# Attention slots beside a matmul stage: transposes and value products set later, evictions issued ahead of conversions, first slots a step later

## The chip, the cores and the metric

The kernel runs on one core of a Trainium2 chip. The metric is the device time of one execution in microseconds (us), the median of several executions. The engines meant below are TensorE (PE, matrix products), VectorE (DVE), ScalarE (ACT), GpSimd (POOL) and SyncE (SP, which here only issues DMAs). Each engine takes its instructions in the order in which they were written for it; semaphores hold an instruction back until its operands are there.

## The reference, cut to what matters

Three blocks follow one another. The first is attention over chunks of 32 queries with 8 memory keys, 16 keys to the left and 8 to the right; the two others are gated products without a nonlinearity. All is float32.

```python
scores = scale * np.matmul(q_c, k_full.transpose(0, 1, 3, 2))
scores = scores - np.max(scores, axis=-1, keepdims=True)
a = np.exp(scores)
a = a / (np.sum(a, axis=-1, keepdims=True) + 1e-09)
out[:, :, c_start:c_end] = np.matmul(a, v_full)
...
a = x @ w1;  b = x @ w2;  h = a * b @ w3;  return h @ w_out          # 3072 tokens, 512 -> 1024 -> 512
...
a = x @ w_a; b = x @ w_b; return (a * b @ w_out)                     # 512 -> 1536 -> 512
```

## The kernel before

**Units and slots.** Attention is cut into 64 units: one batch, 96 queries, half of the heads. A unit `u` goes through eight steps: scores on TensorE (`a_scores`, tile `sc`), the maximum on VectorE (`a_max`, `mx`), the exponentials on ScalarE (`a_exp`, `t`), the normalisation (sums on VectorE, `sm`, and the multiplication on GpSimd, `a_norm`), four transposes on TensorE (`a_trans`, `pt`), their eviction on ScalarE (`a_pt`, tile `p2`, which the traces call `p`), the value product on TensorE (`a_pv`, `xp`, for two units at once, at the odd one) and the split of the result into a high and a low part (`a_x`, `xt`: high on ScalarE, low on VectorE). `slots_of(u)` gives each step a slot number. The scores of unit `u` stand in slot 3u; before the change the transposes stand in slot 3u+5 plus up to six more for the early units, the eviction one slot behind, the value product two behind the transposes (three for units 0 to 9) and the split one more. `attn_slot(n)` issues the next n slots; within a slot the older unit's steps come first. So the slots are one list, and what is written around them decides how they lie among other work.

**Stage one (17 to 96 us): `w3 @ w_out`.** The two weights are multiplied first. Weights come from memory as 64-bit numbers. A call of `w_tick` converts: two scalings of one block on ScalarE (L378, L379) and, for the block before it, three integer operations on VectorE (L383 to L385). Blocks 0 to 7 are needed by steps k = 0 to 7 of the first half; blocks 8 to 11 hold two steps of the second half each. The loop over `order` runs two halves of four PSUM banks (`wps`); in each half steps k = 0 to 5 run over the banks m = 0 to 3, and then steps 6 and 7 bank by bank, and `w_evict` moves each finished bank out (high part on ScalarE, L570, low part on VectorE, L571, tile `wo`). The second half reuses the same four banks in the same order, so its first product into a bank waits for that bank's eviction. After every second product a tick or slots, or both, are issued.

**Stage two (96 to 510 us): the first gated block for 512 tokens at a time, `ti` = 0 to 4 here.** For each of eight feature blocks m, `ab_step` runs 12 matmuls into `psA` and 12 into `psB`; VectorE multiplies the two (`gv`, L635) and ScalarE and GpSimd split the product (`g`). Then come the `psY` products. Between every 12 matmuls `between()` issues first a tick (in `ti` = 0: 16 blocks of `w1` and `w2` are still to be converted, for psA and psB of the coming m) or a step of the preparation of the next weights (tiles `cs`, `co`), and then as many slots as bring the counter to its due value: `NEED[ti]` slots must be out before `ti` starts, since its input `xt` must be complete. There are 24 such places in each `ti`. Before the change 30 or 36 slots fall on them.

**Buffers and queues.** `pt` and `xp` have one buffer each, `p2` has two. Loads of keys, queries and values go through the POOL queue up to unit 13 and through the SP queue afterwards; in the SP queue they stand among the loads of weights and the stores of `co`.

Of the kernel before, what the change touches and what calls it, by code (L numbers as in the profile page):

```python
# [17 lines left out]
GQ = 96  # L18
# [3 lines left out]
TT = 512  # L22
NT1 = B * S // TT
NU = B * NG * 2
NPLAIN = 22
NEARLY = 14
# [9 lines left out]
A0 = (1, 2)  # L36
# [7 lines left out]
def tile_attention_moe(  # L44
# [46 lines left out]
    def mm(o, l, r, first, last):  # L91
        nc.tensor.matmul(o, lhsT=l, rhs=r, start=first, stop=last)  # L92
# [43 lines left out]
    def a_load(u):  # L136
        if u >= NU:
            return
        a_mask(u, queue_of(u))
        a_qk(u, queue_of(u))  # L140
# [7 lines left out]
    def a_prep_hi(u):  # L148
        if u >= NU:
            return  # L150
        q, k = qbuf[u % 2], kbuf[u % 2]
        q2 = att.tile([P, HH, GQ], F32R, tag="q2", name="q2")
        k2 = att.tile([P, HH, 2, KW], F32R, tag="k2", name="k2")
        split_hi(k2[:, :, 0, :], k)
        split_hi(q2[0:D], q[0:D])
        prep[u] = (q2, k2)

    def a_prep_lo(u):
        if u >= NU:
            return  # L160
        q, k = qbuf[u % 2], kbuf[u % 2]
        q2, k2 = prep[u]
        split_lo(k2[:, :, 1, :], k, k2[:, :, 0, :])
        split_lo(q2[D:P], q[0:D], q2[0:D])
# [108 lines left out]


    def trans_slot(u):
        return 3 * u + 5 + max(0, (NEARLY - 2 - u) // 2)

    def slots_of(u):
        t, e = trans_slot(u), int(u < NEARLY - 4)
        return (  # L280
            (t + 3 + e, a_x),
            (t + 2 + e, a_pv),
            (t + 1, a_pt),
            (t, a_trans),
            (3 * u + 3, a_norm),
            (3 * u + 2, a_exp),
            (3 * u + 1, a_max),
            (3 * u, a_scores),
        )

    todo = {}
    for u in range(NU):
        for j, (s, stage_of) in enumerate(slots_of(u)):
            todo.setdefault(s, []).append((j, u, stage_of))
        s = trans_slot(u) - (4 if u < NEARLY - 4 else 1)
        todo.setdefault(s, []).append((len(slots_of(u)), u, a_v))
    acount = [-3]
    NSLOT = 3 * (NU - 1) + 9

    NEED = [3 * (2 * -(-TT * (i + 1) // GQ) - 1) + 9 for i in range(NT1)]  # L300

    def attn_slot(n=1):
        for _ in range(n):
            s = acount[0]
            if s >= NSLOT:
                return
            acount[0] += 1
            for _, u, stage_of in sorted(todo.get(s, []), key=lambda x: x[:2]):
                stage_of(u)

            if s % 3 == 0 and s // 3 + 1 > NPLAIN + 1:
                a_prep_lo(s // 3 + 1)
            if s % 3 == 2 and s // 3 + 2 > NPLAIN + 1:
                a_prep_hi(s // 3 + 2)
            if s % 3 == 0 and NPLAIN <= s // 3 + 1 <= NPLAIN + 1:
                a_prep_hi(s // 3 + 1)
            if s % 3 == 1 and NPLAIN <= s // 3 + 1 <= NPLAIN + 1:
                a_prep_lo(s // 3 + 1)
            if s % 3 == 2:
                if s // 3 + 2 <= NPLAIN + 1:  # L320
                    a_load(s // 3 + 2)
                if s // 3 + 3 >= NPLAIN + 2:
                    a_load(s // 3 + 3)
# [31 lines left out]
    def w_load():  # L355
        i = nload[0]
        if i < len(wsrc):
            tag = "raw64" if size[i] == 1 else "raw2"
            r, x = w_tile(i, tag, [P, size[i] * CH, 2])
            if r is not None:  # L360
                for c in range(2 if i == 0 else 1):
                    n = size[i] * CH // (2 if i == 0 else 1)
                    nc.sync.dma_start(
                        out=r[:, n * c : n * c + n, :].rearrange("p c w -> p (c w)"),
                        in_=wsrc[i][:, 2 * n * c : 2 * n * c + 2 * n],
                    )
                nload[0] += 1
                wraw.append((i, r, tag))
                return True
        return False  # L370

    def w_scale(r):

        l, h = r[:, :, 0], r[:, :, 1].bitcast(F32)
        nc.scalar.activation(h, h, AF.Copy, scale=2.0**-112)  # L378
        nc.scalar.activation(l, l, AF.Copy, scale=2.0**-29)  # L379
# [7 lines left out]
    def halves_of(i, *tiles):  # L387
        if i > 0:
            return [tiles]
        return [[t[:, CH * c : CH * c + CH] for t in tiles] for c in range(2)]  # L390

    def w_sum(i, r):
        kind, f = plan[i][:2]
        if kind == "w12":
            a, ax = w_tile(i, "dec", [P, CH])
            w_bits(a, r)
            return a.bitcast(F32), ax
        if f % 2 == 0:
            pairs["f"] = wpool.tile([P, 2, 2 * CH], U32, tag="w12", name="w3_f")
        a = pairs["f"][:, f % 2, :]  # L400
        for a1, r1 in halves_of(i, a, r):
            w_bits(a1, r1)
        if kind == "w3a":
            w3k[f], wo_f[f] = a[:, :CH], a[:, CH:]
        else:
            w3k[8 + 2 * f], w3k[9 + 2 * f] = a[:, :CH], a[:, CH:]
        return None, None

    def w_tick():

        if len(pipe[2]):
            i, a, ax, (d, f, w, hi, lo) = pipe[2].pop(0)
            nc.vector.tensor_tensor(lo, a, hi.bitcast(F32), ALU.subtract)
            live["dec"][ax] -= 1
            d[f] = w
        if pipe[1]:
            i, a, ax = pipe[1].pop(0)
            t = w_place(*plan[i][:3])
            nc.scalar.activation(t[3], a, AF.Copy)
            pipe[2].append((i, a, ax, t))  # L420
        if len(pipe[0]):
            i, r, tag = pipe[0].pop(0)
            a, ax = w_sum(i, r)
            live[tag][int(tag == "raw2")] -= 1
            if ax is not None:
                pipe[1].append((i, a, ax))
        if wraw:
            i, r, tag = wraw.pop(0)
            for (r1,) in halves_of(i, r):
                w_scale(r1)  # L430
            pipe[0].append((i, r, tag))
        while w_load():
            pass
# [6 lines left out]
    def w_new(pool, tag, n=None):  # L440
        return pool.tile([P, 2, CH], F32R, tag=tag, bufs=n, name=tag)

    def w_place(kind, m, c):

        if c == 0:
            pairs[kind] = wpool.tile([P, 2, 2 * CH], F32R, tag="w12", name="w12")
        w = pairs[kind][:, :, CH * c : CH * (c + 1)]
        v = pairs[kind].rearrange("p l (k j f) -> p l k j f", k=KD, j=2)
        return (w12s if c else {}), m, v, w[:, 0, :], w[:, 1, :]
# [118 lines left out]
    def w_evict(half, m):  # L568
        w = wsm[4 * half + m] = w_new(wpool, "wo")
        nc.scalar.activation(w[:, 0, :], banks[m], AF.Copy)  # L570
        nc.vector.tensor_tensor(w[:, 1, :], banks[m], w[:, 0, :].bitcast(F32), ALU.subtract)  # L571
# [3 lines left out]
    for half in range(2):  # L575
        banks = [psd.tile([P, 512], F32, tag="d", name="wps") for _ in range(4)]
        for k, m in order:
            mm(
                banks[m],
                w3k[8 * half + k].bitcast(F32)[:, P * m : P * m + P],  # L580
                wo_f[k].bitcast(F32),
                k == 0,
                k == 7,
            )
            if k < 6 and m % 2 == 0 or k == 6:
                continue

            if half == 0:
                if m == 1 or k == 7 and m == 3:
                    w_tick()  # L590
                attn_slot(A0[m // 2] * (k > 0) if k < 6 else 1)
            else:
                if k < 6:
                    if m == 3:
                        w_tick()
                    attn_slot(1 + (m == 3 or k % 2 == 0))
                else:
                    if m % 2 == 1:
                        w_tick()
                    if m < 2:  # L600
                        attn_slot()
            if k == 7 and m > 0:
                w_evict(half, m - 1)
        w_evict(half, 3)
    nc.sync.dma_start(out=mask_sb, in_=mask)
    del pairs["f"]
    wo_f.clear()
# [35 lines left out]
    def between():  # L643
# [10 lines left out]
        if ti < NT1 - 1:  # L654
            b = nstep[0] - NB * ti
            attn_slot(NEED[ti] + (NEED[ti + 1] - NEED[ti]) * b // NB - acount[0])

# [49 lines left out]
    for ti in range(NT1):  # L707
        last = ti == NT1 - 1
        gs = {}
        attn_slot(NEED[ti] - acount[0])  # L710
        if last:
# [18 lines left out]
        for n in (0, 2, 1, 3) if last else range(KD):  # L730
            psY = psd.tile([P, 512], F32, tag="d", name="psY")
            i = 0
# [284 lines left out]
```

## Time and profile before

| | before |
|---|---|
| median of 3 runs | 1122.23 us (1122.22, 1122.23, 1123.91) |
| the profiled execution | 1123.84 us, its span 1122.1 us |
| TensorE busy | 1098.8 us, 98% of the span |
| VectorE busy | 642.5 us, 57% |
| ScalarE busy | 515.3 us, 46% |
| GpSimd busy | 310.7 us, 28% |
| chain that ended last | TensorE 80%, VectorE 3%, issue 2%, ScalarE 2%, GpSimd 1% |

TensorE is the bound of the whole, so only its waits count; they are read in the waits of TensorE and in its timeline. An engine that is busy 57% of the span can still bind a stretch, so busy time is read by stretch. The clock that was granted to TensorE (1.00 is 2.4 GHz, 0.50 is 1.2 GHz) is read in the windows: it tells where matmuls ran at half their speed.

### The profile page before, as it was taken

The numbers are of one execution on the slowest core, as the hardware profiler recorded it, in microseconds if no ns is written. First come the engines' busy times: TensorE is split into PE (matmuls) and PEld (weight loads), VectorE is DVE, ScalarE is ACT, GpSimd is POOL, SyncE is SP. The second block draws the span as 40 slices with busy tenths as digits, with TensorE's granted clock in tenths as the row PEclk, the third lists the DMA queues.
The fourth block names the chain that finished last, engine by engine and source line by source line (L and its number), as shares of the span: only waits on it lengthen the run. The fifth ranks groups of instructions, "written<-read, shape, count | busy, mean of one in ns | idle before, by whom it ended". The sixth has DMA issues, their size and how long they took to land.

```text
span 1122.1 us, 15526 instructions
## 1 busy us (share of the span) xinstructions
PE 1098.8 (98%) x5354; PEld 875.6 (78%) x5354; DVE 642.5 (57%) x1342; ACT 515.3 (46%) x1299; POOL 310.7 (28%) x308
## 2 busy tenths in 40 slices
PE   8899999999999999999999999999999999999998
PEld 3466877887787888887877878888888888888887
DVE  6878956877987887864865564252232244222220
ACT  6777656666666756644543334232222223222210
POOL 2452232332332322321212233202233211232210
PEclk9999999999999999999999999999999999999999
DMA  8835445345346345435446455434334352344311
GB/s 298 294 117 163 138 139 185 120 150 171 125 149 196 127 135 160 144 116 197 172 172 229 169 188 187 171 102 169 132 135 180 144 178 89 146 144 185 132 38 37
DMA packets 61671, 174.55 MB, mean 156 GB/s; under 512 B 8022, under 2 KB 18080, under 8 KB 55577
## 3 DMA queue, kind: packets, MB, share of 16 engines
q1 hardware_dynamic: 48762, 102.38, 27.5%
q0 software_dynamic: 12544, 70.91, 17.6%
q8 instruction: 42, 0.69, 0.3%
q14 instruction: 36, 0.29, 0.1%
q10 hardware_dynamic: 287, 0.27, 0.1%
HBM read 139.97 MB, written 33.55 MB: 155 GB/s over the span
## 4 chain that ended last, share of the span: by engine, by line
PE 80%; DVE 3%; issue 2%; ACT 2%; POOL 1%; DMA 0%; DVEq 0%; ACTq 0%; POOLq 0%; SPq 0%
PE ps L803 29%; PE ops L92 17%; PE psY L92 10%; PE psA L92 10%; PE psB L92 10%; PE sc L92 2%; PE xp L92 2%; PE pt L230 1%; DVE dec L384 1%; ACT t L209 0%; POOL t L222 0%; DVE dec L385 0%; DVE xt L146 0%; POOL g L637 0%; ACT xt L143 0%
## 5 line engine op out<-in xcount | busy, mean ns | idle before, releaser
L803 PE MATMUL ps<-x,w 128*128 128x512 f32 x1512 | 349.5, 390 | 3.8 <-ACT tmp L815 3.8
L803 PEld LDWEIGHTS ps<-x,w 128*128 128x128 f32 x1512 | 283.4, 188 | 64.6 <-ACT tmp L815 5.9
L820 DVE TENSOR_TENSOR tmp<-ps,tmp 128x512 f32<-128x512 f32 x108 | 74.6, 691 | 245.0 <-PE ps L803 241.0
L92 PE MATMUL psA<-xt,w 128*128 128x512 f32 x576 | 145.8, 401 | 2.1 <-ACT xt L143 1.5
L702 POOL DMA_DIRECT2D w<-wc x72 | 40.1, 558 | 369.0 <-PE ps L803 368.8
L92 PE MATMUL psB<-xt,w 128*128 128x512 f32 x576 | 141.0, 393 | 0.0
L92 PE MATMUL psY<-g,wo 128*128 128x512 f32 x576 | 139.0, 393 | 0.0
L815 ACT ACTIVATE tmp<-ps 128x512 f32<-128x512 f32 x108 | 64.6, 598 | 146.8 <-PE ps L803 146.8
L222 POOL TENSOR_TENSOR t<-t,sm 96x512 f32<-96x512 f32 x64 | 81.5, 1274 | 175.0 <-ACT k L143 79.8
L92 PEld LDWEIGHTS psA<-xt,w 128*128 128x128 f32 x576 | 106.6, 190 | 26.9 <-ACT xt L143 2.5
L92 PEld LDWEIGHTS psY<-g,wo 128*128 128x128 f32 x576 | 105.6, 188 | 21.0
L92 PEld LDWEIGHTS psB<-xt,w 128*128 128x128 f32 x576 | 105.5, 188 | 20.9
L637 POOL TENSOR_TENSOR g<-gv,g 128x512 fp32r<-128x512 f32 x48 | 67.9, 1414 | 188.6 <-ACT g L636 174.5
L92 PE MATMUL ops<-wo,g 128*128 128x512 f32 x504 | 118.6, 389 | 0.0
L92 PEld LDWEIGHTS ops<-wo,g 128*128 128x128 f32 x504 | 94.6, 188 | 19.6
L826 ACT ACTIVATE g<-tmp 128x512 fp32r<-128x512 f32 x66 | 40.8, 633 | 130.5 <-DVE tmp L825 130.5
L827 POOL TENSOR_TENSOR g<-tmp,g 128x512 fp32r<-128x512 f32 x66 | 87.1, 1342 | 26.5 <-ACT g L826 26.0
L209 ACT ACTIVATE t<-t,mx 96x128 f32<-96x128 f32 x168 | 65.1, 390 | 14.0 <-DVE mx L194 13.9
L92 PE MATMUL ops<-fo,g 128*128 128x512 f32 x288 | 68.2, 389 | 0.0
L92 PE MATMUL wps<-w_f 128*128 128x512 f32 x128 | 60.9, 607 | 4.2 <-DVE w_f L385 2.3
L636 ACT ACTIVATE g<-gv 128x512 fp32r<-128x512 f32 x48 | 30.2, 629 | 72.1 <-DVE gv L635 72.1
L92 PEld LDWEIGHTS ops<-fo,g 128*128 128x128 f32 x288 | 54.1, 188 | 11.2
(83 smaller groups left out, 1318.5 us busy)
## 6 DMA issues: line engine op xcount, KB each, us to landing
w<-wc POOLq DMA_DIRECT2D x36, 1024.0 KB, 6.9
w<-wc POOLq DMA_DIRECT2D x36, 768.0 KB, 4.9
wc<-co SPq DMA_DIRECT2D x84, 256.0 KB, 2.3
raw<-in_wab SPq DMA_DIRECT2D x24, 512.0 KB, 4.3
kraw<-in_kt SPq DMA_DIRECT2D x42, 256.0 KB, 3.2
raw<-in_w SPq DMA_DIRECT2D x16, 512.0 KB, 3.7
raw<-in_w3a SPq DMA_DIRECT2D x7, 1024.0 KB, 9.1
vraw<-in_vw SPq DMA_DIRECT2D x50, 128.0 KB, 2.5
```

Of the source, the lines that this page charges most:

```text
L92: nc.tensor.matmul(o, lhsT=l, rhs=r, start=first, stop=last)
L209: nc.scalar.activation(t[:, h, :], src[:, h, :], AF.Exp, bias=mx[:, h : h + 1], scale=scale, accum_out=sm[:, h : h + 1],)
L222: nc.gpsimd.tensor_tensor(t, t, sm[:, :, None].to_broadcast([GQ, HH, KW]), ALU.mult)
L230: nc.tensor.transpose(pt[:, h, :], t[:, h, :], id_sb)
L636: nc.scalar.activation(g2[:, 0, :], gv, AF.Copy)
L637: nc.gpsimd.tensor_tensor(g2[:, 1, :], gv, g2[:, 0, :].bitcast(F32), ALU.subtract)
L702: nc.gpsimd.dma_start(out=t[:, c0:c1].bitcast(F32), in_=src[:, c0:c1])
L803: nc.tensor.matmul(ps, lhsT=w[:, i, a, k, :], rhs=xs[i][:, b, k, :], start=first and n == 0, stop=n == 5, skip_group_check=not first,)
L815: nc.scalar.activation(z, ps, AF.Copy)
L820: nc.vector.tensor_tensor(z, ps, y, ALU.add)
L826: nc.scalar.activation(g2[:, 0, :], z, AF.Copy)
L827: nc.gpsimd.tensor_tensor(g2[:, 1, :], z, g2[:, 0, :].bitcast(F32), ALU.subtract)
```

## The change

`trans_slot` puts the transposes of units 12 and up six slots behind their scores instead of five. `slots_of` now sets the value product three slots behind the transposes and the split four behind for all units but 10 and 11; before, that held for units 0 to 9 only, and the others had two and three. `NSLOT` and `NEED` follow from the table: each `NEED` but the first grows by two, so 32 slots instead of 30 fall into `ti` = 0 and the split that ends a block of tokens stays in the last slot before its due time. In stage one the slots start at k = 2 instead of k = 1, three slots later; the second half issues two slots at each place, 24 in the k < 6 part instead of 21, so the counter is the same (42) at its end. `w_evict` of a bank is issued in front of the tick and the slots of its place instead of behind them, and the second tick at the end of the first half stands behind the last eviction.

```diff
     def trans_slot(u):
-        return 3 * u + 5 + max(0, (NEARLY - 2 - u) // 2)
+        n = NEARLY - 2
+        return 3 * u + (6 if u >= n else 5 + (n - u) // 2)
     def slots_of(u):
-        t, e = trans_slot(u), int(u < NEARLY - 4)
+        t, e = trans_slot(u), int(u // 2 != NEARLY // 2 - 2)
...
-    NSLOT = 3 * (NU - 1) + 9
-
-    NEED = [3 * (2 * -(-TT * (i + 1) // GQ) - 1) + 9 for i in range(NT1)]
+    NSLOT = max(todo) + 1
+    NEED = [slots_of(2 * -(-TT * (i + 1) // GQ) - 1)[0][0] + 1 for i in range(NT1)]
...
+            if k == 7 and m > 0:
+                w_evict(half, m - 1)
             if half == 0:
-                if m == 1 or k == 7 and m == 3:
+                if m == 1:
                     w_tick()
-                attn_slot(A0[m // 2] * (k > 0) if k < 6 else 1)
+                attn_slot(A0[m // 2] * (k > 1) if k < 6 else 1)
             else:
                 if k < 6:
                     if m == 3:
                         w_tick()
-                    attn_slot(1 + (m == 3 or k % 2 == 0))
+                    attn_slot(2)
...
-            if k == 7 and m > 0:
-                w_evict(half, m - 1)
         w_evict(half, 3)
+        if half == 0:
+            w_tick()
```

VectorE at the seam of the two halves of stage one, before (`raw_275`, `raw_312`: blocks 9 and 10 of the weights; `wo<-wps`: evictions; `mx`, `sm`: maximum and sums of a unit):

```order
L571 TENSOR_TENSOR wo<-wps,wo 128x512
L383 TENSOR_SCALAR w_f<-raw_275 128x1024
L384 SCALAR_TENSOR_TENSOR w_f<-raw_275,w_f 128x1024
L385 ISA w_f<-raw_275,w_f 128x2048
L220 TENSOR_SCALAR sm<-sm 96x4
L221 RECIPROCAL sm<-sm 96x4
L571 TENSOR_TENSOR wo<-wps,wo 128x512 x2
L186 TENSOR_REDUCE mx<-sc 96x4
L187 TENSOR_SCALAR mx<-mx 96x4
```

VectorE at the same seam, now (`raw_254` is block 9):

```order
L571 TENSOR_TENSOR wo<-wps,wo 128x512 x2
L220 TENSOR_SCALAR sm<-sm 96x4
L221 RECIPROCAL sm<-sm 96x4
L571 TENSOR_TENSOR wo<-wps,wo 128x512
L383 TENSOR_SCALAR w_f<-raw_254 128x1024
L384 SCALAR_TENSOR_TENSOR w_f<-raw_254,w_f 128x1024
L385 ISA w_f<-raw_254,w_f 128x2048
L186 TENSOR_REDUCE mx<-sc 96x4
L187 TENSOR_SCALAR mx<-mx 96x4
```

The last evictions stood behind the conversion of block 9 and stand ahead of it now; the maximum, of unit 6 before and of unit 5 now, stands behind that conversion in both.

ScalarE at this seam, before (`p_446` is the evicted transposes of unit 3):

```order
L570 ACTIVATE wo<-wps 128x512 x2
L234 ACTIVATE p_446<-pt 128x384
L209 ACTIVATE t,sm<-sc,mx 96x128 x4
L378 ACTIVATE raw_366<-raw_366 128x1024
L379 ACTIVATE raw_366<-raw_366 128x1024
```

ScalarE, now (`p_454` is the evicted transposes of unit 3, `p_423` those of unit 2):

```order
L570 ACTIVATE wo<-wps 128x512 x2
L378 ACTIVATE raw_286<-raw_286 128x1024
L379 ACTIVATE raw_286<-raw_286 128x1024
L143 ACTIVATE xt<-xp 128x4x96
L234 ACTIVATE p_423<-pt 128x384
L209 ACTIVATE t,sm<-sc,mx 96x128 x4
L378 ACTIVATE raw_341<-raw_341 128x1024
L379 ACTIVATE raw_341<-raw_341 128x1024
L234 ACTIVATE p_454<-pt 128x384
```

The eviction of unit 3's transposes stood right behind the last bank evictions; now two scalings of a block and the exponentials of unit 5 are between them.

ScalarE in `ti` = 0, before (`p_1159` is unit 15's eviction, `g_1091` the split of the product of m = 3):

```order
L209 ACTIVATE t,sm<-sc,mx 96x128 x4
L234 ACTIVATE p_1159<-pt 128x384
L636 ACTIVATE g_1091<-gv 128x512
L419 ACTIVATE w_1139<-dec 128x512
L378 ACTIVATE raw_1113<-raw_1113 128x512
L379 ACTIVATE raw_1113<-raw_1113 128x512
```

ScalarE in `ti` = 0, now (`p_1192` is unit 15's eviction, `g_1096` the split of m = 3):

```order
L638 ACTIVATE g_1096<-gv 128x512
L419 ACTIVATE w_1146<-dec 128x512
L378 ACTIVATE raw_1118<-raw_1118 128x512
L379 ACTIVATE raw_1118<-raw_1118 128x512
L234 ACTIVATE p_1192<-pt 128x384
L209 ACTIVATE t,sm<-sc,mx 96x128 x4
L633 ACTIVATE av<-psA 128x512
```

Unit 15's eviction stood ahead of the split of m = 3 and stands behind it now, and behind a tick's three activations.

TensorE in `ti` = 0, now, at the value product that reads it (`w_982` is m = 4):

```order
L92 MATMUL psB<-xt,w_982 128x512 x12
L92 MATMUL xp<-p_1086,vraw 64x96 x4
L92 MATMUL xp<-p_1192,vraw 64x96 x4
L230 MATMUL pt<-id_sb,t 128x96 x4
L92 MATMUL sc<-kraw,qraw 96x128 x4
L92 MATMUL psA<-xt,w_1052 128x512 x12
```

Before, that product stood behind psA of m = 4 and alone; now value product, transposes and scores stand together behind psB of m = 4.

## Rows read from the trace of the kernel before

**Rows 1.** Waits of TensorE, whole span: us in total, times, longest.

```profile
PE pt L230 <- POOL t L222: 2.3, 3, 1.3
PE xp L92 <- ACT p L234: 2.2, 1, 2.2
PE sc L92 <- DMA qraw<-in_qt: 2.2, 1, 2.2
PE wps L92 <- DVE wo L571: 1.9, 1, 1.9
PE psA L92 <- ACT xt L143: 1.5, 3, 0.6
PE pt L230 <- ACT p L234: 0.9, 1, 0.9
```

**Rows 2.** Windows: length, PE, PEld, DVE, ACT, POOL busy, granted clock, DMA, GB/s.

```profile
17.00:42.00 25.00, 21.89 (x87) 11.92 (x86) 23.10 (x35) 19.31 (x47) 11.32 (x17) 1.00 0.88 302
94.00:141.00 47.00, 44.77 (x237) 35.77 (x236) 43.90 (x75) 32.84 (x84) 11.64 (x10) 0.96 0.45 143
56.00:59.00 3.00, 3.00 (x10) 1.09 (x10) 2.90 (x5) 2.20 (x9) 1.91 (x3) 0.50 0.55 187
114.00:117.00 3.00, 3.00 (x9) 2.35 (x8) 2.87 (x5) 1.84 (x4) 1.64 (x2) 0.50 0.69 224
```

**Rows 3.** Timeline of TensorE: start, us, line, instruction, count, idle before.

```profile
32.47 1.08 PE L92 MATMUL sc<-kraw,qraw 67*96 67x128 f32 x8 [2.20 <-DMA qraw<-in_qt]
...
55.35 3.20 PE L92 MATMUL wps<-w_f 128*128 128x512 f32 x4 [1.94 <-DVE wo L571]
...
60.97 1.88 PE L92 MATMUL wps<-w_f 128*128 128x512 f32 x4
62.69 0.50 PE L230 MATMUL pt<-id_sb,t 96*128 96x96 f32 x4
...
67.46 0.88 PE L92 MATMUL xp<-p,vraw 128*64 128x96 f32 x16
...
157.73 3.00 PE L92 MATMUL psY<-g,wo 128*128 128x512 f32 x12
```

**Rows 4.** Timeline of VectorE at the seam of the two halves.

```profile
51.23 0.68 DVE L383 TENSOR_SCALAR w_f<-raw 128x1024 uint32<-128x1024 uint32 x1
...
54.64 1.25 DVE L571 TENSOR_TENSOR wo<-wps,wo 128x512 fp32r<-128x512 f32 x2
55.81 0.68 DVE L186 TENSOR_REDUCE mx<-sc 96x4 f32<-96x512 f32 x1
```

**Rows 5.** Timeline of ScalarE at the same seam.

```profile
53.48 0.53 ACT L234 ACTIVATE p<-pt 128x384 f32<-128x384 f32 x1
56.80 0.36 ACT L209 ACTIVATE t<-sc,mx 96x128 f32<-96x128 f32 x1 [2.79 <-DVE mx L187]
...
58.19 1.16 ACT L378 ACTIVATE raw<-raw 128x1024 f32<-128x1024 f32 x1
```

**Rows 6.** Timeline of VectorE in `ti` = 0: the product of m = 3.

```profile
130.47 0.68 DVE L635 TENSOR_TENSOR gv<-psB,av 128x512 f32<-128x512 f32 x1
```

**Rows 7.** Timeline of ScalarE around it.

```profile
129.87 0.49 ACT L234 ACTIVATE p<-pt 128x384 f32<-128x384 f32 x1
131.18 0.63 ACT L636 ACTIVATE g<-gv 128x512 fp32r<-128x512 f32 x1 [0.82 <-DVE gv L635]
...
132.24 0.65 ACT L378 ACTIVATE raw<-raw 128x512 f32<-128x512 f32 x1
```

**Rows 8.** Timeline of TensorE at the seam of `ti` = 0 and 1.

```profile
180.45 0.63 PE L92 MATMUL sc<-k,q 128*96 128x256 f32 x4
...
183.75 0.88 PE L92 MATMUL xp<-p,vraw 128*64 128x96 f32 x16
184.56 0.55 PE L230 MATMUL pt<-id_sb,t 96*128 96x96 f32 x4
185.52 3.43 PE L92 MATMUL psA<-xt,w 128*128 128x512 f32 x12 [0.42 <-ACT xt L143]
```

## The prediction

> **What bounds the kernel now.** I read the waits of TensorE first, because TensorE is busy nearly all the time and only its waits can be won. Those that the change can touch sum to 11.0 us: transposes for GpSimd 2.3, a value product for ScalarE 2.2, scores for a load 2.2, a bank for its eviction 1.9, psA for its input 1.5, a transpose for ScalarE 0.9 [rows 1]. Then the windows: behind the eviction wait and behind the value product wait the granted clock is 0.50 (1.2 GHz) for some 3.4 us [rows 2], of which I show 3 us each; half speed over 3.4 us loses 1.7 us. So about 14.5 us hang on these waits. Next, the other engines in the same stretches: VectorE is busy 23.1 of 25 us between 17 and 42 us, and 43.9 of 47 us between 94 and 141 us [rows 2]. That is the point to see: the waits of TensorE lie just where VectorE has nearly no idle time. A wait that another full engine causes cannot be removed by an order alone; it can only move.
>
> Times below count from the start of the profiled span (1122.1 us; that execution took 1123.84 us, so 1.7 us lie around the span). The three timed runs stand at 1122.2, 1122.2 and 1123.9, a distance of one such stretch at half clock, so the profile belongs to the upper kind.
>
> **Stage one.** What moves: slots start one step later, evictions go ahead of ticks, 24 slots instead of 21 in the second half. No instruction is added or removed. I follow VectorE and ScalarE, with these prices: a conversion on VectorE 3.2 (from 51.23 to the sums and evictions that end at 55.81) [rows 4], an eviction 0.6 [rows 4], a maximum 0.8 (up to 1.2 at some), sums 0.3, exponentials 1.4 to 1.5 [rows 5], the two scalings of a block 2.1 to 2.3 [rows 5], the eviction of transposes 0.5 [rows 5].
>
> VectorE begins block 4 at 22.4, when its scaling is done, as before. Blocks 4 to 7 with three maxima and two sums (12.9 + 3.2 + 0.6) end at 39.1. Sums and the maximum of unit 3 follow (40.6), then its exponentials (42.3), its transposes' eviction (42.8), bank 0's eviction on ScalarE and VectorE (44.05), block 8 (47.3), the maximum of unit 4 (48.1), its exponentials (49.75), the evictions of banks 2 and 3 (51.9). TensorE asks for banks 2 and 3 at 51.4 and 52.3: **the eviction wait of 1.94 goes**, with a margin of 0.4.
>
> What is late next stands on the order of ScalarE. Block 9 ends at 55.15, the maximum of unit 5 behind it at 55.95, its exponentials at 57.6, the scalings of the tick behind them at 59.7, and only then comes the eviction of unit 3's transposes, done at 60.2. Before, that eviction ran at 53.48 [rows 5]. TensorE wants it for the value product of units 2 and 3 at 57.0: two products take 1.72 [rows 3], eight pairs of them, four scores, four transposes and one value product from the late scores of unit 3 (36.4) on. So **a new wait of about 3.2 us** follows the removed one. The scores' wait for their load does not go either: the load stands in the POOL queue behind a normalisation whose sums come 3.9 us later (a conversion and a maximum are ahead of them), and TensorE comes only 3.4 us later (the four products that now go ahead), so 2.2 becomes some 2.7 to 3.0. Small waits of 0.3 to 0.9 follow at two transposes. By the third value product I count 69.65 against 67.46 before [rows 3], with two products (1.72) more behind it: **0.5 us behind**, although before had a stretch at half clock there. The bounds: 1.5 us ahead if only half of the new waits comes, 1.2 us behind if the new wait drops the clock, of whose 1.7 the waits that follow absorb about 1.
>
> From 70 us on TensorE waits for nothing in both, until the first psA at 96.5. VectorE, though, reaches its last eviction about 1.1 us later than before (99.9 for 98.8), since the maximum of unit 11 stands behind a tick now; 0 to 2 us is what I allow.
>
> **`ti` = 0.** Here the lengthened distances act: the value product that waited 2.2 [rows 1] now stands two places behind its eviction, and the transposes that waited 1.3 have a slot more. Both waits go, and with the clock's 1.7 this is 5.3 us. But VectorE works through the same list without a gap up to gv of m = 3, which began at 130.47 [rows 6]; 1.1 later it is 131.6. Unit 15's eviction ran at 129.87, ahead of the split of that product [rows 7]; now it stands behind the split and a tick. From gv: split at 132.3, one more activation and two scalings (131.18 to 132.24 for the first two, 0.65 for a scaling), eviction 134.5 to 135.0 [rows 7]. TensorE, without its old waits, asks for it at 130.3 (ten times 2.83 us of psA or psB from 96.5, four transposes, four scores, a value product). So **a wait of 4.7 us** stands where 5.3 were won, and a clock at half speed behind it is likely: 1.94 and 2.23 us of idle were each followed by one, while 2.20 us at 32.47 was not [rows 2, 3]. From that product on TensorE again binds: the first psY at 157.4, or at 159.1 with the clock's loss, against 157.73 [rows 3]. I take 159.1, **1.4 behind**.
>
> The Trainium skill ("TensorE: Matmul & The Clock Gate", section "Why this matters for your kernels") advises against idle gaps of several us between bursts, since the clock falls behind them. The rows show it falling after shorter gaps too, and not after each, so length alone doesn't decide; by the page as by my choice the 4.7 us gap costs a stretch, and the sum would be the same.
>
> **After `ti` = 0.** The two other transposes' waits, 0.95 together (2.3 less 1.3 [rows 1]), go, with three slots between normalisation and transposes. At a seam of two `ti` the split follows the value product, and psA waits for it: value product at 183.75, transposes at 184.56, psA at 185.52, with 0.42 shown as wait and another 0.4 inside its first twelve (3.43 for 2.9 to 3.0) [rows 8]. Now scores stand behind the transposes there, 0.47 each [rows 8]. They cover that much at four of the five seams: 1.9. Together **2.8 us**, with bounds 0 (ScalarE may be late with the split, having exponentials ahead) and 3.5.
>
> The costs I set at nothing: the loads of values in the SP queue come one slot later and now stand two slots, not three, behind the product that frees their buffer; stores wait behind them, and TensorE's distance to what those stores free covers it. If that cover goes, see the second rival. The table's other buffers keep their distances.
>
> **The sum.** 159.1, plus the rest of the span as before (1122.1 less 157.7, 964.4), less 2.8, is 1120.7; with 1.7 around the span 1122.4. Against the median of 1122.23 this is no change; a measurement of this kernel tells about 0.2% (2.2 us) from none.
>
> **The rivals.** (1) The waits go and come back smaller. Without the half clock behind the new wait in `ti` = 0 the sum is 1120.7, and with VectorE not 1.1 late 1119.6. If VectorE were no bound at all, the 14.5 us go outright: 1109. For it: TensorE may run up to 8 us ahead of VectorE's weights in `ti` = 0. Against: the order puts unit 15's eviction behind gv. Chance of under 1120.0: 0.30. (2) Slower: the SP queue. A value load that waits for TensorE holds back the stores of `co`, and ScalarE, in order, waits for their buffer with evictions behind it. Some 20 loads wait up to a slot (2.3 us) longer; it decides if ScalarE falls more than two slots behind TensorE. If one in four costs 0.8, this is 4 us, 1126.4. With both new waits' half clock and no gain at the seams 1125.2 comes out by another way. Together over 1124.5: 0.20. (3) The eviction wait stays, for lack of 0.4 us of margin: under 1 us, and inside the forecast.
>
> **How the numbers follow.** Forecast (no change): 0.50, its own range 1120.0 to 1124.5. Faster 0.30, slower 0.20. The range from 1117.5 to 1125.5 takes in the missing half clock, the bounds of VectorE's lag and half of the slower cases; it leaves out some 0.1 on each side.
>
> **What would show it.** Right: no wait of wps for wo; a wait of 2.5 to 4 us of xp for ScalarE near 57 to 60 us and one of 3 to 5 us near 130 to 135, a clock of 0.50 behind at least one; VectorE over 90% busy from 94 to 141; no waits of transposes for GpSimd; psA's waits at the seams shorter. Wrong: no wait of xp over 1 us before 157 us (then the time is below 1118), or ScalarE waiting longer for the stores of `co` and TensorE for ScalarE after 200 us (then above 1124).

## The result and the profile after

| | before | after |
|---|---|---|
| median, same chip | 1123.47 us (6 runs) | 1130.82 us (6 runs) |
| ratio | | 1.0072, 95% interval 1.0062 to 1.0083 |
| the profiled execution, its span | 1123.84, 1122.1 us | 1132.6, 1130.8 us |
| TensorE busy | 1098.8 us | 1102.1 us |
| first psA of `ti` = 0 | 96.54 us | 97.61 us |
| first psY of `ti` = 0 | 157.73 us | 159.15 us |
| from there to the end of the span | 964.4 us | 971.6 us |

The change makes the kernel slower by 0.7%, outside the predicted range of 1117.5 to 1125.5. The last three lines tell where: up to the first psY the two kernels stand 1.4 us apart, and behind it 7.3 us more are lost. The waits of TensorE after (as in [rows 1]; us in total, times, longest):

```profile
PE psY L92 <- ACT g L638: 3.4, 1, 3.4
PE xp L92 <- ACT p L234: 3.0, 1, 3.0
PE psY L92 <- POOL g L639: 2.6, 3, 1.0
PE sc L92 <- DVE mx L194: 2.3, 4, 0.6
...
PE sc L92 <- DMA qraw<-in_qt: 2.0, 2, 1.6
...
PE sc L92 <- DVE mx L187: 1.6, 1, 1.6
...
PE pt L230 <- POOL t L222: 0.8, 1, 0.8
```

The eviction wait is gone, the waits of transposes for GpSimd went from 2.3 to 0.8, and the value product waits once, 3.0 us, in stage one. New are waits of psY for `g` of ScalarE and of GpSimd, 6.0 us together, and scores that wait for a maximum. Where they stand, in the timeline of TensorE after (as in [rows 3]):

```profile
35.06 1.08 PE L92 MATMUL sc<-kraw,qraw 67*96 67x128 f32 x8 [1.57 <-DVE mx L187]
...
59.08 0.77 PE L92 MATMUL xp<-p,vraw 128*64 128x96 f32 x8 [3.02 <-ACT p L234]
...
127.56 1.99 PE L92 MATMUL sc<-kraw,qraw 67*96 67x128 f32 x8 [1.60 <-DMA qraw<-in_qt]
...
322.99 4.96 PE L92 MATMUL psY<-g,wo 128*128 128x512 f32 x21
331.34 0.50 PE L92 MATMUL psY<-g,wo 128*128 128x512 f32 x1 [3.38 <-ACT g L638]
332.86 1.22 PE L92 MATMUL psY<-g,wo 128*128 128x512 f32 x2 [1.02 <-POOL g L639]
...
357.89 2.98 PE L92 MATMUL psA<-xt,w 128*128 128x512 f32 x12
```

And the windows of after (as in [rows 2]: length, PE, PEld, DVE, ACT, POOL busy, granted clock, DMA, GB/s):

```profile
94.00:141.00 47.00, 44.60 (x230) 35.17 (x229) 43.89 (x76) 33.29 (x91) 11.25 (x9) 0.93 0.51 151
...
59.50:66.00 6.50, 6.50 (x25) 4.10 (x22) 4.69 (x7) 3.36 (x12) 5.01 (x8) 0.50 0.33 100
128.00:134.00 6.00, 6.00 (x19) 4.99 (x18) 5.67 (x10) 4.72 (x15) 1.43 (x3) 0.50 0.52 160
332.50:339.00 6.50, 6.14 (x19) 5.07 (x20) 6.30 (x19) 4.70 (x17) 1.63 (x2) 0.50 0.14 49
...
320.00:340.00 20.00, 15.60 (x76) 12.16 (x75) 19.18 (x53) 13.56 (x43) 6.01 (x6) 0.83 0.38 131
```

The last of these windows, before:

```profile
320.00:340.00 20.00, 20.00 (x125) 16.08 (x124) 18.26 (x53) 12.29 (x42) 5.76 (x4) 1.00 0.39 132
```

TensorE ran at 1.2 GHz behind the waits at 59.08, 127.56 and 331.34, for some 6.8 us each, where before had two such stretches of 3.4 us. From 320 to 340 us VectorE is busy 19.18 of 20 us while TensorE stands still for 4.4; before, TensorE was busy all of these 20 us. So 6.8 of the 7.3 us lie in one place: the psY products of `ti` = 2 took 34.9 us from the first psY to the next `ti` (322.99 to 357.89), before 28.1 (321.58 to 349.65). All other parts behind 159 us differ by 1 us or less each.

The order in which VectorE and ScalarE work there repeats with every pair of psA and psB in `ti` = 2. VectorE after (start, us, line, instruction, idle before it):

```profile
276.44 0.68 DVE L637 TENSOR_TENSOR gv<-psB,av 128x512 f32<-128x512 f32 x1
...
310.43 0.17 DVE L220 TENSOR_SCALAR sm<-sm 96x4 f32<-96x4 f32 x1 [0.23 <-ACT t L209]
...
310.95 0.69 DVE L146 TENSOR_TENSOR k<-kraw,k 128x512 fp32r<-128x512 f32 x1
311.68 1.28 DVE L146 TENSOR_TENSOR q<-qraw,q 64x384 fp32r<-64x384 f32 x1
312.99 0.56 DVE L146 TENSOR_TENSOR xt<-xp,xt 128x384 fp32r<-128x384 f32 x1
313.46 0.68 DVE L190 TENSOR_TENSOR t<-sc,mask_sb 96x512 f32<-96x512 f32 x1
...
315.02 0.68 DVE L637 TENSOR_TENSOR gv<-psB,av 128x512 f32<-128x512 f32 x1
...
317.95 0.17 DVE L220 TENSOR_SCALAR sm<-sm 96x4 f32<-96x4 f32 x1 [1.91 <-ACT t L209]
...
329.94 0.68 DVE L637 TENSOR_TENSOR gv<-psB,av 128x512 f32<-128x512 f32 x1
```

ScalarE after, in the same stretch:

```profile
315.74 0.63 ACT L638 ACTIVATE g<-gv 128x512 fp32r<-128x512 f32 x1 [2.88 <-DVE gv L637]
316.27 0.39 ACT L209 ACTIVATE t<-t,mx 96x128 f32<-96x128 f32 x1
...
322.80 0.63 ACT L638 ACTIVATE g<-gv 128x512 fp32r<-128x512 f32 x1 [1.96 <-DVE gv L637]
```

To read them together: sums, low parts of keys and queries, split, maximum, gv on VectorE; gv lets ScalarE make `g`; the exponentials stand behind `g`; and the sums wait for the exponentials. **These steps stand in one chain, each behind the one before**: from 310.43 to 317.95 one turn takes 7.5 us. VectorE waits 1.91 us in this turn; in others the preparation of the weights (`co`, `dec`) fills that time, and it is busy 47.7 of the 53.5 us from the first gv to the last. The eight gv of `ti` = 2 begin at 276.44 to 329.94, 7.6 us apart; before, they were 7.2 apart. TensorE's pair takes 6.95 (55.6 us from first psA to first psY, by 8), so it runs ahead until it needs the last `g`. Before, the exponentials stood ahead of `g` on ScalarE and ran beside VectorE's work on gv, and gv waited for TensorE twice, at 272.11 and at 314.30 (VectorE before):

```profile
302.09 0.68 DVE L635 TENSOR_TENSOR gv<-psB,av 128x512 f32<-128x512 f32 x1
308.78 0.68 DVE L635 TENSOR_TENSOR gv<-psB,av 128x512 f32<-128x512 f32 x1
314.30 0.69 DVE L635 TENSOR_TENSOR gv<-psB,av 128x512 f32<-128x512 f32 x1 [0.97 <-PE psB L92]
```

What made the round is `NEED`: 72, 102, 138 before, multiples of three, and 74, 104, 140 after. `ti` = 2 has 36 slots for 24 places, so one place takes one slot and the next two. Before, the place behind psA took scores and sums (slot 3u) and the one behind psB the maximum and the exponentials; after, the exponentials (3u+2) stand alone behind psA, and sums, scores and maximum all stand behind psB, ahead of gv.

### The profile page after: what moved, and what is told of

Read it like the earlier page. It is cut to its first block, busy times and chain, and to the rows that moved or that the text cites. A ratio compares the mean times of both kernels' runs of the same rounds, so it can differ in the third digit from the quotient of the medians.

```text
span 1130.8 us, 15527 instructions
## 1 busy us (share of the span) xinstructions
PE 1102.1 (97%) x5354; PEld 880.4 (78%) x5354; DVE 652.0 (58%) x1342; ACT 515.7 (46%) x1299; POOL 313.3 (28%) x308
## 4 chain that ended last, share of the span: by engine, by line
PE 66%; DVE 11%; ACT 7%; issue 5%; DMA 1%; POOL 1%; SPq 0%; DVEq 0%; ACTq 0%; POOLq 0%
PE ps L805 29%; PE ops L92 17%; PE psY L92 9%; PE psA L92 5%; PE psB L92 4%; ACT t L209 3%; DVE q L146 2%; DVE gv L637 1%; DVE t L190 1%; DVE t L194 1%; DVE dec L384 1%; PE sc L92 1%; ACT k L143 1%; DVE co L146 1%; PE pt L230 1%
## 5 line engine op out<-in xcount | busy, mean ns | idle before, releaser
L92 PE MATMUL psA<-xt,w 128*128 128x512 f32 x576 | 143.5, 398 | 1.5 <-DVE xt L146 0.9
L222 POOL TENSOR_TENSOR t<-t,sm 96x512 f32<-96x512 f32 x64 | 85.1, 1330 | 196.5 <-ACT k L143 100.2
L92 PEld LDWEIGHTS psY<-g,wo 128*128 128x128 f32 x576 | 108.3, 191 | 29.5 <-ACT g L638 3.8
```

Source lines behind the costliest of these rows:

```text
L222: nc.gpsimd.tensor_tensor(t, t, sm[:, :, None].to_broadcast([GQ, HH, KW]), ALU.mult)
```

## The experiments

All times are medians against the kernel before on the same chip. "Behind psY" is the span less the start of the first psY of `ti` = 0; "`ti` = 2" runs from its first psA to that of `ti` = 3. Both are read from the timeline of TensorE in the one profiled execution of each run, so they need not add up to the ratio; that of the run with the table, NEED + 1 and evictions in front took 1124.20 us, 4.6 above its median. NEED + 1 means that each due value but the first is one later.

| run | ratio, 95% | first psY | behind psY | `ti` = 2 |
|---|---|---|---|---|
| before | | 157.73 | 964.4 | 84.2 |
| after | 1.0072 [1.0062, 1.0083] | 159.15 | 971.6 | 90.5 |
| table alone | 1.0047 [1.0034, 1.0059] | 155.98 | 971.4 | 90.3 |
| stage one alone | 1.0029 [1.0017, 1.0040] | 159.34 | 964.5 | 84.3 |
| after, NEED + 1 | 1.0000 [0.9991, 1.0009] | 160.22 | 962.2 | 84.0 |
| before, NEED + 2 | 1.0015 [1.0007, 1.0024] | 155.82 | 966.8 | 87.3 |
| table, NEED + 1 | 0.9979 [0.9970, 0.9988] | 155.64 | 961.9 | 84.0 |
| after, gv first | 1.0333 [1.0315, 1.0351] | 161.15 | 996.0 | 89.0 |
| after, places swapped | 1.0068 [1.0055, 1.0081] | 158.16 | 970.1 | 88.2 |
| table, NEED + 1, evictions in front | 0.9971 [0.9963, 0.9980] | 157.62 | 964.8 | 84.5 |
| the same, seam slots first | 0.9934 [0.9921, 0.9948] | 158.95 | 957.4 | 81.7 |
| after, queries on GpSimd | 0.9999 [0.9990, 1.0008] | 157.49 | 963.1 | 82.0 |

**The table alone, stage one alone.** The diff of the change, split in two: `trans_slot`, `slots_of`, `NSLOT` and `NEED` in the one, the loop of stage one in the other.

> The new table of slots (and NEED, NSLOT by it) with stage one as before. Three theories on the 7.3 us that are lost behind the first psY (971.65 us from there to the end, 964.3 before). RING: each NEED behind the first grew by two, so another third of the slots now falls on the place behind psA; between two gv VectorE's sums, splits and maximum, ScalarE's g and its exponentials then wait for one another in one ring of some 7.5 us, longer than the 6.9 us of the pair psA and psB in ti = 2. DISTANCE: transposes, value product and scores now stand in one slot, and this heap costs, wherever the places are. CARRIED: the lag comes from stage one and is never made up. RING and DISTANCE: 1128 to 1131 us, behind the first psY 970 to 972, psY waiting for g of ScalarE by some 3 us near 331. CARRIED: 1122 to 1125, 964 to 966 behind the first psY.

> The edits of stage one alone (first slots one step later, evictions in front), with the table of slots as before. RING and DISTANCE: 1121 to 1125 us, from the first psY to the end 963 to 966, no psY waiting for g by over 1 us. CARRIED: 1128 to 1131, 970 to 972 behind the first psY. By all three no wait of wps for wo near 55, and a wait of xp for ScalarE of about 3 us near 59.

The table alone took 1127.61 us (1122.83 for before) and has the wait of psY for `g` (3.4 us), with TensorE 1.8 us *earlier* at the first psY than before; the edits of stage one alone took 1126.01 without that wait. So nothing is carried over from stage one, and CARRIED falls. One number missed: stage one alone came out 1 us above what I wrote. Its span is only 1.7 us longer than that of the profiled execution of before, and each has one stretch at half clock in stage one (before at 56 to 59 us [rows 2]). Two other runs with stage one as before had none there and reached the first psA at 94.9 and 95.3 us; with the edited stage one it is 97.1 to 98.2 in six runs. The edits cost 2 to 3 us against an undisturbed stage one, and the clock accounts for about as much: the six have 3.4 to 10.2 us at 0.50 there, which is 1.7 to 5.1 us lost.

**The due values one and two later.** After, with the due values multiples of three again:

```diff
     NEED = [slots_of(2 * -(-TT * (i + 1) // GQ) - 1)[0][0] + 1 for i in range(NT1)]
+    NEED = [n + (i > 0) for i, n in enumerate(NEED)]
```

and before, with the values of the change (the same line with `n + 2 * (i > 0)`, the table as it was).

> The changed kernel with each NEED but the first raised by one (75, 105, 141, 171): the distances of the table stay, and the slots stand at the places behind psA and psB as before the change, since the due values are multiples of three again. RING: 1121 to 1125 us, 962 to 966 behind the first psY, no wait of psY for g over 1 us near 331. DISTANCE and CARRIED: 1128 to 1132, 970 to 972 behind the first psY.

> The kernel before with each NEED but the first raised by two (74, 104, 140, 170, as the change has them): old distances, stage one as before, the other third of the slots behind psA. RING: 1126 to 1131 us, 968 to 972 behind the first psY, and in ti = 2 gv of VectorE and g of ScalarE wait for each other in turn. DISTANCE and CARRIED: 1121 to 1125, 963 to 966 behind the first psY.

The first is as RING said: 1122.65 us, 962.2 behind psY, no wait of psY for ScalarE. The distances are those of the change, so DISTANCE falls. The second speaks against RING by its time, 1124.39 us, which the two others allowed, and for none by the 966.8 us behind psY. But its trace has the round of the kernel after (ScalarE and VectorE, before with NEED + 2):

```profile
311.14 0.63 ACT L637 ACTIVATE g<-gv 128x512 fp32r<-128x512 f32 x1 [3.38 <-DVE gv L636]
...
313.35 0.17 DVE L220 TENSOR_SCALAR sm<-sm 96x4 f32<-96x4 f32 x1 [1.91 <-ACT t L209]
```

but TensorE is held back by it in small pieces, at value products two slots behind their transposes (TensorE, the same run):

```profile
284.33 0.55 PE L92 MATMUL xp<-p,vraw 128*64 128x96 f32 x8 [0.21 <-ACT p L234]
300.07 0.55 PE L92 MATMUL xp<-p,vraw 128*64 128x96 f32 x8 [1.80 <-ACT p L234]
316.27 0.55 PE L92 MATMUL xp<-p,vraw 128*64 128x96 f32 x8 [0.72 <-ACT p L234]
```

2.7 us in three waits, and `ti` = 2 takes 3.1 us more than before. The gv stand 7.7 us apart, as after. Behind the wait of 1.80 the clock fell as well, for some 3.4 us (its window, the same run):

```profile
301.00:304.00 3.00, 3.00 (x8) 2.34 (x7) 2.07 (x11) 1.20 (x3) 0.49 (x1) 0.50 0.01 5
```

From 320 to 340 us it stays at 1.00. So the round comes from the due values with either table, at a price of some 3 us; RING as I had written it was too simple. With the distances of the change the value products don't wait, so the lag is passed to TensorE only at psY, at once, and the clock falls behind that wait, for twice as long.

**Does it add up, and two edits meant to open the round.** The table and NEED + 1 with stage one as before; after, with gv and `g` issued ahead of the slots behind psB; after, with the due slots of `ti` = 2 rounded up, so that the place behind psA takes two slots and that behind psB one:

```diff
-        between()
         nc.vector.tensor_tensor(gv, psB[:, :TT], av, ALU.mult)
         ...
+        between()
```

```diff
-            attn_slot(NEED[ti] + (NEED[ti + 1] - NEED[ti]) * b // NB - acount[0])
+            attn_slot(NEED[ti] + ((NEED[ti + 1] - NEED[ti]) * b + (NB - 1) * (ti == 2)) // NB - acount[0])
```

> Stage one as before, the new table, each NEED but the first one later than the table gives it (75, 105, 141, 171). The runs so far: the table alone costs 4.8 us, stage one's edits alone 3.2, table and stage one with the later NEED nothing. If the costs add, as RING says (the later NEED takes the wait of psY for g away, whatever stage one does): 1118 to 1121 us, first psY at 155 to 157 us, 964 or less from there to the end. If the later NEED only helps where TensorE comes late from stage one (OFFSET: what counts is how far TensorE stands from VectorE, not which place a slot has): 1123 to 1128, with a wait of psY for g of 2 to 4 us near 328.

> The changed kernel with gv and its split g issued ahead of the slots behind psB instead of behind them. RING: gv no longer stands behind sums, splits and maximum, so exponentials and g no longer wait for one another: no wait of psY for g of ScalarE near 331, and 1122 to 1126 us. ScalarE now holds its evictions of transposes behind g while psB runs, up to 3 us, so waits of xp for p may come instead; with those on every pair as in the run with the old table and NEED two later (4.6 us in all), 1126 to 1129. OFFSET: as the changed kernel, 1129 to 1132.

> The changed kernel with the due slots of ti = 2 rounded up instead of down: the place behind psA takes two slots and that behind psB one, where it was one and two; nothing else moves. RING: this alone takes the ring apart (sums, splits of keys and queries behind psA, maximum behind psB with nothing but the split of xp ahead of it): ti = 2 takes 84 to 85 us instead of 90.5, 1123 to 1126 us. If the loss in ti = 2 is brought in from ti = 1 or from due values that are too early (OFFSET), ti = 2 stays at 88 or more and the time at 1128 to 1132.

The first came out as the sum: 1120.31 us against 1123.15, faster than both kernels; OFFSET falls, since TensorE arrives early here (155.64) and no psY waits for ScalarE. The other two missed what I had expected by RING, but the traces show that neither edit opened the round. With gv first the wait of psY for ScalarE shrinks to 0.2 us, and another round closes: gv waits for `av` (1.92 us at 306.34), which stands on ScalarE behind the exponentials, these wait for the maximum, and the maximum now stands behind gv. The gv are 7.9 us apart, scores wait for the maximum, 18.7 us in 14 waits, and `ti` = 1 to 3 take 5 to 9 us longer than before. With the places swapped VectorE and ScalarE keep the very order of the round, sums, low parts, maximum, gv, `g`, exponentials, sums; only TensorE's scores moved ahead of psB (VectorE, ScalarE and TensorE, places swapped):

```profile
314.12 0.68 DVE L637 TENSOR_TENSOR gv<-psB,av 128x512 f32<-128x512 f32 x1
...
317.04 0.17 DVE L220 TENSOR_SCALAR sm<-sm 96x4 f32<-96x4 f32 x1 [1.91 <-ACT t L209]
...
314.84 0.63 ACT L638 ACTIVATE g<-gv 128x512 fp32r<-128x512 f32 x1 [3.20 <-DVE gv L637]
...
314.34 0.69 PE L92 MATMUL sc<-k,q 128*96 128x256 f32 x4 [1.66 <-DVE mx L194]
329.25 0.68 PE L92 MATMUL sc<-k,q 128*96 128x256 f32 x4 [1.19 <-DVE mx L194]
```

The eight gv stand 7.8 us apart (274.24 to 329.03). The wait at psY of `ti` = 2 is gone, but TensorE meets the same round at the scores: from unit 22 on `sc` has one buffer, so the scores of a unit need the maximum of the one before. `ti` = 2 gained only 2.3 of 6.3 us. VectorE is busy just 44.8 of the 54.8 us between the first gv and the last, so a VectorE with too much to do doesn't explain the distance of the gv; the round does.

**The length of the round.** After, and for the twelve units whose scores fall into `ti` = 2 a step of 1.28 us of VectorE's part of the round goes to GpSimd; no other instruction moves:

```diff
-        split_lo(q2[D:P], q[0:D], q2[0:D])
+        if NEED[2] <= 3 * u < NEED[3]:
+            nc.gpsimd.tensor_tensor(q2[D:P], q[0:D], q2[0:D].bitcast(F32), ALU.subtract)
+        else:
+            split_lo(q2[D:P], q[0:D], q2[0:D])
```

> The changed kernel; for the twelve units whose scores fall into ti = 2 the low part of the queries (1.28 us on VectorE) is computed on GpSimd instead. The order of everything else stays. RING, in the form that the runs left: the round sums, splits of keys and queries, maximum, gv on VectorE, then g and exponentials on ScalarE takes 7.1 to 7.9 us, TensorE's pair some 6.9, so 1.28 less makes it shorter than TensorE's: no wait of psY for g of ScalarE near 331, ti = 2 takes 83.5 to 85.5 us instead of 90.5, 1123 to 1126 us. If the wait comes from anything but the length of that round (the heap of value product, transposes and scores in one place, a load, a store): ti = 2 stays above 88 us and the time at 1128 to 1132.

1122.68 us against 1122.66, 8.1 less than after; `ti` = 2 takes 82.0 us, less than the 83.5 that I had put as its lower end, and the time lies 0.3 under its range too. The gv of this run stand 6.9 us apart (274.25 to 322.64), no psY waits for ScalarE, and the clock stays at 1.00 (its window):

```profile
320.00:340.00 20.00, 19.75 (x112) 15.97 (x110) 15.08 (x50) 13.51 (x44) 9.16 (x8) 1.00 0.47 155
```

The order of the change with a round shorter than TensorE's pair loses nothing behind psY (963.1 us, 964.4 before). The heap of value product, transposes and scores, the loads and the stores stand where they stood, so they were not the cause. VectorE has less to do here as well (15.08 of 20 us); that this alone was not it is told by the run with the places swapped. Together they show the cause: the length of the round.

**Evictions in front, and the seam.** The table, NEED + 1 and, of stage one's edits, only the evictions issued in front; then also, at the last place of each `ti`, the slots ahead of the step of the weights' preparation:

```diff
         nstep[0] += 1
+        if ti < NT1 - 1 and nstep[0] == NB * (ti + 1):
+            attn_slot(NEED[ti + 1] - acount[0])
         if any(pipe) or wraw:
```

> As the run of stage one as before with the new table and the later NEED, and the bank evictions of stage one issued in front of the ticks and slots of their place, without the other edits of stage one (first slots and last tick where they were). What this tells is which edit of stage one costs the 3.2 us: if it is the later slots (the exponentials and scalings that come ahead of an eviction of transposes), this is 0 to 2 us faster than that run, without the wait of wps for wo of 1.9 to 2.0 near 55; if it is the evictions in front (they move the transposes' eviction back), it is 1.5 to 3.5 us slower than that run, with a wait of xp for ScalarE of 2 to 3.5 us near 57 to 60.

> The last run's kernel (stage one as before but for the evictions in front, the new table, the later NEED), and at the last place of each ti the slots issued in front of the step of the weights' preparation instead of behind it. In that run psA waited 2.3 us at 186.36 and 2.2 us at 351.96 for the split xt of ScalarE, and half clock followed; ScalarE came to that split late, since the step in front of it (co) waited up to 2.7 us for its buffer's store. If that is the cause, both waits go, with up to 1.7 us of half clock at each: 1114 to 1118 us. If the split is late for its own reasons (the value product, the exponentials ahead of it): 1118.5 to 1121, waits as they were.

The evictions in front cost nothing and gain little: 1119.59 us, an interval that overlaps that of the run without them, and the wait of wps for wo, which I had expected to go, went only from 2.0 to 1.5. So the 3 us that stage one's edits cost should come from the later slots and the moved tick, but no run has these alone. One trace doesn't tell 2 us here: this run and the next have the same stage one and reached the first psA at 95.06 and 97.51, with 3.4 and 6.8 us at half clock there. The seam was a wait for a store (ScalarE, evictions in front):

```profile
351.33 0.42 ACT L143 ACTIVATE co<-dec 128x256 fp32r<-128x256 f32 x1 [2.76 <-DMA wc<-co]
351.65 0.53 ACT L143 ACTIVATE xt<-xp 128x128 fp32r<-128x128 f32 x2
```

and the psA that waits for this split, in TensorE's timeline of the same run:

```profile
351.96 4.78 PE L92 MATMUL psA<-xt,w 128*128 128x512 f32 x12 [2.16 <-ACT xt L143]
```

With the slots first no psA waits at a seam, and the kernel takes 1116.29 us, 0.66% less than before and, by the two ratios, 1.4% less than the change; of all runs it is the fastest.

## Why the prediction was wrong, step by step

- **Stage one: right in kind.** The eviction wait went; xp waited 3.02 us at 59.08 (predicted 3.2 at 60.2). Where I had the scores wait 2.7 to 3.0 for their load, they waited 1.57 for a maximum (35.06), and for a load only 0.39, at 40.34; the 1.60 at 127.56 is in `ti` = 0. The clock fell behind the new wait and stayed down for 6.8 us, so the third value product came at 70.61, not 69.65, and the first psA 1.07 us late, inside the bound of 1.2.
- **`ti` = 0: right sum, wrong place.** The first psY came at 159.15 (predicted 159.1), with VectorE busy 43.89 of 47 us. VectorE's lag was 2.1 us, not 1.1 (last eviction done at 101.0, before 98.9), and gv of m = 3 began at 132.36 (predicted 131.6). But the wait of 4.7 us at unit 15's product isn't there. TensorE waited 0.80 for GpSimd and 1.60 for a load at 127.56, ran at half clock, and came late enough to find the eviction done. In the run with the queries on GpSimd the clock stayed up in this stretch, and there the product does wait and starts at 135.28 (predicted 135.0), but after 1.57 us instead of 4.7; of the 3.1 that are missing, waits ahead of it took 2.0 (0.82 for GpSimd, 1.20 for the load).
- **After `ti` = 0: this step failed.** I wrote 2.8 us gained, bounds 0 and 3.5; 7.3 were lost, and with the 10 us between them the sum fails. I counted which waits of TensorE the new distances remove and took over the rest of the span. The section on the change says that each `NEED` grows by two, and I read it as 32 slots for 30 in `ti` = 0; that in `ti` = 1 to 4 the same number of slots now falls one or two residues of three later, on other places, I didn't follow. The lower bound of zero came from ScalarE at the seams alone. Of the terms themselves, the transposes' waits for GpSimd behind `ti` = 0 went, but the seams gave little: psA waits 1.5 us in all, as before. Where the round is open, the number comes near, 961.9 and 962.2 us behind psY, 2.2 to 2.5 less than before, but by luck: psA waits at the seams rose to 3.6 and 3.9 us, and the gain lies in the eight pairs of `ti` = 2 (54.0 us from first psA to first psY, before 56.1).
- **The rivals.** Slower was to come from the SP queue: ScalarE's waits for stores of `co` between 155 and 515 us went from 36.0 to 24.3 us, so that wasn't it, though the same wait cost the seams of the later run. Of what was to show the forecast wrong, "TensorE for ScalarE after 200 us" came, from another cause. Too much of the chance, 0.80, lay on not slower, since no case had the round in it.

## What to carry to other kernels

When slots of a fixed cycle are laid on places by a rounded formula, a shift of the count by one or two changes which steps share a place, even if no distance changes: write out, for each stage, what one engine does between two of its products on the main path, and follow the dependences round until they close. If the loop's length exceeds TensorE's time for the same work, the lag grows with every turn. Here it showed as one wait at the end, far from the edit, or as small waits on the way where TensorE needed something of the loop earlier. To move steps to other places doesn't open the loop as long as the engines in it keep their order, as the run with the places swapped shows; to shorten it below TensorE's time did.

## What the runs showed of the hardware

**The clock.** Before, 1.94 and 2.23 us of idle time were followed by 3.4 us at 0.50. After, the three stretches at 0.50 behind 3.02, 1.60 and 3.38 us lasted 6.8 us, so each cost about 3.4 us, twice what I had put in, and the shortest of the three waits (with another of 0.80 two us ahead of it) cost as much as the others. The length of a wait doesn't tell its price: in the run of the table with NEED + 1, 2.10 us at 347.02 were followed by some 3.4 us at 0.50, 2.00 us at 55.22 by none; nor did the clock fall behind the 1.57 us at 35.06 after.

**A VectorE operation beside GpSimd.** The low part of the queries (64x384) took 1.28 us in 34 of 42 units after, and 0.55 in the other 8; all 34 overlap GpSimd's normalisation, none of the 8 does. Six of the 8 overlap GpSimd's part of `g`, which starts behind them, and keep their 0.55. VectorE and GpSimd, after:

```profile
318.47 0.69 DVE L146 TENSOR_TENSOR k<-kraw,k 128x512 fp32r<-128x512 f32 x1
319.19 1.28 DVE L146 TENSOR_TENSOR q<-qraw,q 64x384 fp32r<-64x384 f32 x1
...
318.49 1.57 POOL L222 TENSOR_TENSOR t<-t,sm 96x512 f32<-96x512 f32 x1 [0.76 <-ACT k L143]
```

The keys start first and take their 0.69; the normalisation starts just behind them; and the queries end 0.41 us behind it, as if they had waited until then. 0.73 us of each turn of the round are this, about the 0.7 by which the gv stand further apart than TensorE's pairs. Of the seven between the first gv of `ti` = 2 and the last, all took 1.28 after; three took 0.55 before and four in the run of after with NEED + 1, so a part of what the due values cost may run through this. The Trainium skill ("SBUF — State Buffer", section "Who interferes with whom") has VectorE and GpSimd take one pair of ports by an exclusive lock; these rows agree with it, but no run here took the overlap alone away.
